# Attention into a token-and-channel mixer on one core: three numbers of the planner that orders TensorE's work

## The chip, the core and the metric

The kernel runs on one core of one Trainium2 chip. The time is that of the device, in microseconds, for one execution of the whole kernel; smaller is better. The number compared is the median of several executions. A core has TensorE (PE: matrix products), VectorE (DVE), ScalarE (ACT), GpSimd (POOL) and SyncE (SP). Here GpSimd issues the loads, SyncE issues the transposes made by DMA and the stores. Matrix products write to PSUM, which VectorE and ScalarE read; everything else lives in SBUF.

## The reference, cut to what matters

```python
# q, k, v: (8 batches, 12 heads, 448 rows, 64)
scores = scale * (q @ k.T) - log(448)
attn = 1 / (1 + exp(-scores))            # a sigmoid in place of a softmax
x = (attn @ v), heads side by side       # (8, 448, 768)
h = relu(x.T @ w_tok1) @ w_tok2          # token mixing: 448 -> 256 -> 448
u = x + h.T
h2 = relu(u @ w_ch1) @ w_ch2             # channel mixing: 768 -> 1536 -> 768
out = u + h2                             # float32
```

## The kernel before, in words

The eight batches run through the same steps. The names below are those of the planner's units, and the lines those of the profile.

*Attention* of a batch is three groups of four heads. The unit S (scores, L578: eight matmuls for a pair of units) is followed by a sigmoid on ScalarE (L594); V (values, L616, 28 matmuls) sums over the 448 keys. Scores and values use 64 x 64 tiles of the array. From batch 2 on, q and k are loaded by GpSimd, permuted (L496) and turned by a DMA transpose (L501), and the attention's result goes back to row order by a DMA transpose (L664, "x"; a part of batches 2 and 3 goes through TensorE, L675).

*Token mixing.* V1 and K1 (L841, L857) make the hidden layer, K2 and V2 (tok2, L933 and L891) the sum back over rows. VectorE adds x (L955, L923) and so makes u in float32. ScalarE casts each block of u to float16 (L963), and SyncE turns it with a DMA transpose into uT (L991); there are four of these for a batch, named uT_b_0 to uT_b_3, the last block shared by two batches.

*Channel mixing.* C1 (L1007) has 12 units of six matmuls of 448 columns, VectorE applies the relu (L1023). C2 (L1066) has six or eight units of twelve matmuls of 384 columns; VectorE adds u (L1079), SyncE stores (L1050, L1044). The first C1 unit of a batch, C1_b_0, needs all four uT of the batch, since a matmul of it takes all rows as the moving operand.

Each C1 and C2 unit is made of two halves, a first one and one whose name ends in "_h". Both write the same PSUM bank, so a unit is open until its second half is done. A unit is "broken" when other work stands between the halves.

*What sets the order.* A planner in the kernel's Python code (class Plan, L55 to L218) computes the order before the program is built. It keeps its own estimates of durations and of landing times, walks through time, and asks `choose` (L1153) at each step which unit TensorE takes next. `choose` gathers candidates that are ready by these estimates and takes the one with the lowest priority number: a group of scores that is due has 1, one not yet due has 5; the token units have 2, C1 has 3, C2 has 4, tails (V1, V2) 3.5. The first K2 of a pair has 4.5 while the counter `rest`, the microseconds of TensorE mixer work since the last K2, is under REST (L1197). A second half has its own number (L1201). When a score group is due is given by `due` (L1135): a share of the mixer work of the batch before, less LEAD microseconds. Engines then execute their own instructions in the order written; semaphores carry the true dependencies, so the planner's estimates decide the order alone and not when something may start.

Of the kernel before, what the change touches and what calls it, by code (L numbers as in the profile page):

```python
# [55 lines left out]
class Plan:  # L56
# [75 lines left out]
    def run(self, choose):  # L132

        lists = {}
        for o in self.ops:
            if o.engine != "PE":
                lists.setdefault(o.engine, []).append(o)
        free = dict.fromkeys([*lists, "PE", "POOL"], 0.7)
        free["POOL"] = 0.8
        mode = [None]  # L140
        self.left = len(self.ops)
        while self.left:
            best = None
            for e, ops in lists.items():
                if e == "LD":
                    ops = ops[:1]
                for o in ops:
                    r = self.ready(o)
                    if r is None:
                        continue  # L150
                    at = free[e]
                    if e == "LD":
                        at = max(free["POOL"], self.landed[-8])
                    key = (max(r, at), o.rank, r)
                    if best is None or key < best[0]:
                        best = (key, e, o)
            pick = choose(self, free["PE"])
            if pick is not None:
                t, ops, kind = pick
                if best is None or t <= best[0][0]:  # L160
                    for o in ops:
                        r = self.ready(o)
                        t = max(t, r, free["PE"])
                        if kind != mode[0]:
                            t += 0.1
                            mode[0] = kind
                        self.hold(o)
                        o.start, o.end = t, t + o.us
                        free["PE"] = t = o.end
                        self.log.append(o)  # L170
                        self.left -= 1
                    continue
            if best is None:
                raise RuntimeError(
                    "\n".join(
                        f"{o.name} <- {[d.name for d in o.after if d.end is None]}"
                        for o in self.ops
                        if o.start is None
                    )[:1500]
                )  # L180
            (t, _, _), e, o = best
            self.hold(o)
            o.start = t
            if e == "LD":
                far = self.load_far if self.pipe > 50.0 else 0.4
                free["POOL"] = t + o.n * o.issue
                self.pipe = max(self.pipe, free["POOL"] + 1.3) + o.us
                while self.hitch and self.pipe > self.hitch[0][0]:
                    self.pipe += self.hitch.pop(0)[1]
                o.end = self.pipe + far  # L190
                self.landed += [o.end] * o.n
            elif e == "SP":
                free[e] = t + o.us
                o.end = t + self.far + min(5.0, max(0.0, self.pipe - t - 0.5))
            else:
                o.end = free[e] = t + o.us
            lists[e].remove(o)
            self.log.append(o)
            self.left -= 1
        self.log.sort(key=lambda o: o.start)  # L200
        for o in self.log:
            o.emit()
# [3 lines left out]
def kernel(  # L206
# [23 lines left out]
    DH = D // 2  # L230
    att_scale = 1.0 / math.sqrt(E)
    att_bias = -math.log(S)
    LEAD, SPAN, REST, LATE = 20.0, 0.86, 0.8, 0
    FILL, UP, SURE = 21.0, 7, 0.8
    PACK, PACK2 = range(2, 8), range(2, 8)
    JOIN, PULL, ALONE = 0.05, 3.0, 3.5
# [898 lines left out]
    def due(g):  # L1135
        b, i, _ = g
        return -1.0 if b < 2 else base[b - 1] - LEAD + i * SPAN * mix[b - 1]

    def settle():
        c = state["chosen"]  # L1140
        state["chosen"] = None
        if c is None or c[2][0].start is None:
            return
        row = c[4]
        row.remove(c[5])
        if any(o.name[:3] == "V2_" for o in c[2]):
            state["rest"] = -PAUSE
        if row is not groups and c[2][0].name[0] != "V":
            o = c[2][0]
            state["done"] += o.us  # L1150
            state["rest"] = 0.0 if o.name[:2] == "K2" else state["rest"] + o.us

    def choose(plan, t):  # L1153
        settle()
        tails[:] = [o for o in tails if o.start is None]
        g = groups[0] if groups else None
        plan.spare = g is None or len(g[2]) < 3 or state["done"] < due(g) - 1.5
        cands = []
        want = groups[0][2] if groups and groups[0][0] and state["done"] >= due(groups[0]) else []
        late = [d.end for o in want for d in o.after]  # L1160
        short = want and None not in late and max(late) < t + 0.5 and want[0].name[0] == "V"
        for o in extra:
            r = plan.ready(o)
            if r is not None:
                cands.append((max(r, t), o.pri, [o], o.kind, extra, o))
        if groups:
            g = groups[0]
            r = plan.ready(*g[2])
            if r is not None:
                more = []  # L1170
                for o in tails[:3]:
                    r2 = plan.ready(*g[2], *more, o) if g[0] else None
                    if r2 is not None and r2 <= max(t, r) + JOIN:
                        more.append(o)
                        r = max(r, r2)
                p = -1 if g[0] == 0 else 1 if state["done"] >= due(g) - (PULL if more else 0) else 5
                cands.append((max(t, r), p, g[2] + more, "64", groups, g))
        if tails and (ALONE or not groups):
            alone = []
            for o in tails[:3]:  # L1180
                r = plan.ready(*alone, o)
                if r is not None and r <= t + 0.3:
                    alone.append(o)
            if alone:
                cands.append((max(t, plan.ready(*alone)), ALONE or 1.5, alone, "64", [0], 0))
        for rank, kinds in ((2, K), (3, C1), (4, C2)):
            n = 0
            for row in kinds:
                for o in row:
                    if o.name[:2] == "K2" and o.name[-1] == "1" and row.index(o) > 0 and row[row.index(o) - 1].name[:-1] == o.name[:-1]:  # L1190
                        n += 1
                        continue
                    r = plan.ready(o)
                    if short and rank == 2:
                        r = None
                    if r is not None:
                        p = 4.5 if o.name[:2] == "K2" and o.name[-1] == "0" and state["rest"] < REST else rank  # L1197
                        if o.name[:4] == "K2_0":
                            p = 3.5
                        if o.name[-2:] == "_h":  # L1200
                            p = 1.2  # L1201
                        cands.append((max(r, t), p, [o], "128", row, o))
                    n += 1
                    if n > (3 if rank == 2 else 0):
                        break
                if n > (3 if rank == 2 else 0):
                    break
        o = fill.get("op")
        if o is not None and o.start is None:
            plan.ops.remove(o)  # L1210
            uT[0].users.remove(o)
            plan.left -= 1
            fill["op"] = None
        if 3.0 < t < FILL and (not cands or min(c[0] for c in cands) > t + 0.12) and up.start is not None:
            if any(x <= t - SURE for x, _ in plan.free_slots("bank", up)):
                o = fill["op"] = filler()
                plan.left += 1
                state["chosen"] = (t, 0, [o], "128", [o], o)
                return t, [o], "128"
        if not cands:  # L1220
            return None
        first = min(c[0] for c in cands)
        cands = [c for c in cands if c[0] <= max(first, t) + 0.06]
        c = min(cands, key=lambda c: (c[1], c[0]))
        state["chosen"] = c
        return c[0], c[2], c[3]

    with tc.manual_schedule():
        plan.run(choose)
# [30 lines left out]
```

## Time and profile before

| | |
|---|---|
| median of 5 executions | 376.39 us |
| lowest and highest | 375.44 and 382.24 us |
| the profiled execution | 382.24 us, its span 380.4 us |
| granted TensorE clock in it | 0.986 of full speed |
| TensorE busy | 369.1 us (97%) |
| ScalarE, VectorE, GpSimd busy | 208.1, 175.6, 116.1 us |
| read from and written to HBM | 43.45 and 11.01 MB |

The profiled execution is the slowest of the five. The span runs from the first to the last instruction; the executions' time has some 1.8 us around it. A "busy" TensorE is not one at its peak, and shares of busy time are averages over stages with different limits. A wait names the engine or DMA that came last. In SyncE's rows a transpose's length is the time of issuing it, and the transfer lands later.

### The profile page before, as it was taken

How to read it: one execution, taken by the hardware profiler on the slowest of the kernel's cores; microseconds unless marked ns; L12 is line 12 of the kernel's file. 1: busy time of each engine (PE TensorE's matmuls, PEld its weight loads, DVE VectorE, ACT ScalarE, POOL GpSimd, SP SyncE). 2: the span in 40 equal slices, each digit the busy share in tenths (PEclk: the TensorE clock that was granted, in tenths of full speed). 3: DMA queues.
4: the chain of work that ended last, by engine and by line, in shares of the span. 5: the costliest groups of instructions: out<-in, count | busy, mean ns of one | idle time of the engine just before them, and what ended most of it. 6: DMA issues, size and time to landing. Idle time of an engine off the chain costs nothing.

```text
span 380.4 us, 7967 instructions
## 1 busy us (share of the span) xinstructions
PE 369.1 (97%) x3188; PEld 187.5 (49%) x3188; DVE 175.6 (46%) x414; ACT 208.1 (55%) x269; POOL 116.1 (31%) x261
## 2 busy tenths in 40 slices
PE   8799999999999999999699999999999999999995
PEld 4355345554444544455244555445455555555653
DVE  4366345743334644353124463664462257755222
ACT  5787993286777767788357576762665321200000
POOL 8882236234544435444424433440000000000000
PEclk9989999999999999999789999999999999999999
DMA  6999999499899989999989799994013563400344
GB/s 102 174 174 206 211 206 183 86 157 213 126 142 139 196 158 121 134 129 194 205 144 122 119 156 186 158 192 97 17 26 74 110 135 92 86 0 2 83 98 110
DMA packets 97013, 50.06 MB, mean 132 GB/s; under 512 B 70544, under 2 KB 93456, under 8 KB 96976
## 3 DMA queue, kind: packets, MB, share of 16 engines
q1 hardware_dynamic: 72656, 27.62, 40.8%
q0 software_dynamic: 24080, 21.62, 40.8%
q8 instruction: 25, 0.41, 0.5%
q10 hardware_dynamic: 240, 0.31, 0.2%
q14 instruction: 12, 0.10, 0.1%
HBM read 43.45 MB, written 11.01 MB: 143 GB/s over the span
## 4 chain that ended last, share of the span: by engine, by line
PE 92%; DMA 3%; POOL 2%; ACT 1%; DVE 0%; issue 0%; ACTq 0%; POOLq 0%
PE c L1007 30%; PE c L1066 29%; PE qk L578 11%; PE xa L616 8%; PE yn L933 4%; PE k L857 3%; DMA uT<-u 2%; DMA q<-in_q_dram 2%; POOL k L329 1%; PE xb L675 1%; PE k L707 1%; ACT attn L594 1%; POOL q L329 1%; PE k L817 1%; PE k L841 1%; PE tq L524 1%
## 5 line engine op out<-in xcount | busy, mean ns | idle before, releaser
L594 ACT ACTIVATE attn<-qk,att_bias 128x896 f16<-128x896 f32 (+1 forms) x172 | 161.8, 987 | 67.1 <-PE qk L578 66.3
L1007 PE MATMUL c<-uT,w_ch 128*128 128x448 f16 x576 | 121.8, 358 | 3.1 <-DMA uT<-u 3.1
L1066 PE MATMUL c<-w_ch,h2aT 128*128 128x384 f16 x576 | 100.0, 326 | 0.0
L1023 DVE TENSOR_SCALAR h2aT<-c 128x384 f16<-128x384 f32 x96 | 53.5, 557 | 85.0 <-PE c L1007 84.9
L1007 PEld LDWEIGHTS <-w_ch 128*128 128x128 f16 x576 | 53.1, 99 | 61.3 <-issue 15.4
L1066 PEld LDWEIGHTS <-h2aT 128*128 128x128 f16 x576 | 54.8, 98 | 40.6 <-issue 5.9
L1079 DVE TENSOR_TENSOR u<-u,c 128x384 f32<-128x384 f32 x48 | 26.6, 554 | 67.4 <-PE c L1066 67.1
L578 PE MATMUL qk<-qT,kT 64*64 64x448 f16 x672 | 54.3, 368 | 0.9 <-ACT attn L594 0.3
L781 POOL COPY mark<-attn 1x1 f16<-1x1 f16 x54 | 9.7, 180 | 91.7 <-ACT attn L594 91.6
L616 PE MATMUL xa<-attn,v 64*64 64x448 f16 x672 | 36.9, 351 | 0.0
L963 ACT ACTIVATE u<-u 128x768 f16<-128x768 f32 x21 | 17.7, 844 | 28.9 <-DVE u L955 28.7
L578 PEld LDWEIGHTS <-kT 64*64 64x64 f16 x672 | 14.8, 105 | 32.8 <-issue 30.7
L955 DVE TENSOR_TENSOR u<-x,yn 128x384 f32<-128x384 f16 x48 | 24.6, 548 | 4.8 <-PE yn L933 4.7
L496 POOL COPY kp<-k 128x384 f16<-128x384 f16 (+1 forms) x54 | 21.3, 429 | 16.9 <-DMA k<-in_k_dram 14.6
L653 ACT ACTIVATE xT<-xa 128x448 f16<-128x448 f32 (+2 forms) x61 | 22.2, 440 | 7.2 <-PE xa L616 5.7
L616 PEld LDWEIGHTS <-v 64*64 64x64 f16 x672 | 19.8, 108 | 12.2 <-issue 0.9
L496 POOL COPY qp<-q 128x384 f16<-128x384 f16 (+1 forms) x54 | 21.4, 433 | 8.5 <-DMA q<-in_q_dram 8.2
L933 PE MATMUL yn<-h,w_tok 128*128 128x384 f16 x104 | 21.6, 327 | 0.0
L1023 DVE TENSOR_SCALAR h2odd<-c 128x64 f16<-128x64 f32 x96 | 20.6, 214 | 0.0
L1066 PE MATMUL c<-w_ch,h2odd 128*128 128x384 f16 x96 | 17.1, 326 | 0.0
L340 POOL DMA_DIRECT2D q<-in_q_dram x21 | 15.1, 718 | 6.4 <-issue 5.3
L340 POOL DMA_DIRECT2D k<-in_k_dram x21 | 15.1, 719 | 4.7 <-issue 4.7
(73 smaller groups left out, 207.1 us busy)
## 6 DMA issues: line engine op xcount, KB each, us to landing
out_dram<-u SPq DMA_DIRECT2D x48, 192.0 KB, 3.1
k<-in_k_dram POOLq DMA_DIRECT2D x21, 224.0 KB, 5.1
q<-in_q_dram POOLq DMA_DIRECT2D x21, 224.0 KB, 5.5
v<-in_v_dram POOLq DMA_DIRECT2D x21, 224.0 KB, 5.5
w_ch<-in_moe_w_ch_dram POOLq DMA_DIRECT2D x6, 768.0 KB, 18.4
out_dram<-ut SPq DMA_DIRECT2D x6, 192.0 KB, 3.6
v<-in_v_dram POOLq DMA_DIRECT2D x6, 112.0 KB, 5.1
x<-xT SPq DMA_TRANSPOSE x32, 4.1
```

The source lines that it names most:

```text
L340: nc.gpsimd.dma_start(out=t.ap().rearrange("r h j e -> r h (j e)"), in_=heads.rearrange("(h s) (p j) e -> (s p) h (j e)", s=2, j=J),)
L496: nc.gpsimd.tensor_copy(out=pm[:, to, :, :], in_=src[:, fr, :, :])
L578: nc.tensor.matmul(out=ps[64 * s : 64 * s + 64, h, 0:S], lhsT=kT[64 * h : 64 * h + 64, i, s, :], rhs=qT[64 * h : 64 * h + 64, :, s, :], st ...
L594: nc.scalar.activation(out=at[:, hs, :], in_=ps[:, hs, 0:S], func=SIGMOID, bias=bias_t[:, :], scale=att_scale,)
L616: nc.tensor.matmul(out=ps[s](slice(64 * h, 64 * h + 64)), lhsT=vf[64 * s : 64 * s + 64, h, order[i], :], rhs=attn[i][64 * s : 64 * s + 64, ...
L653: nc.scalar.activation(out=xt[:, s, to : to + n], in_=ps[s](every)[:, fr : fr + n], func=COPYF)
L933: nc.tensor.matmul(out=ps[:, :], lhsT=w_tok2[:, t, s0 : s0 + 2, :], rhs=h1[b][:, t, c], start=(t == 0), stop=(t == 1),)
L955: nc.vector.tensor_tensor(out=to, in0=x, in1=y, op=ADD)
L1007: nc.tensor.matmul(out=ps[:, :], lhsT=w_ch1[cb // 4][:, db, 128 * (cb % 4) : 128 * (cb % 4) + 128], rhs=uT[b][:, db, :], start=(db == 0), ...
L1023: nc.vector.tensor_scalar(out=to, in0=ps[:, fr], scalar1=0.0, scalar2=None, op0=MAX)
L1066: nc.tensor.matmul(out=ps[:, :], lhsT=h, rhs=w, start=(cb == 0), stop=(cb == NCB - 1))
L1079: nc.vector.tensor_tensor(out=t, in0=t, in1=ps[:, :], op=ADD)
```

## The change

Three numbers of the planner and the length of an error text are changed. LEAD goes from 20 to 18, so that score groups fall due later by 2 us of mixer work. REST goes from 0.8 to 1.0. The priority of a second half goes from 1.2, ahead of all but due score groups, to 2.1, behind the token units (2) and ahead of the start of another C1 unit (3) or C2 unit (4).

```diff
@@ class Plan, run
-                    )[:1500]
+                    )[:200]
@@ the kernel's constants
-    LEAD, SPAN, REST, LATE = 20.0, 0.86, 0.8, 0
+    LEAD, SPAN, REST, LATE = 18.0, 0.86, 1.0, 0
@@ choose
                         if o.name[-2:] == "_h":
-                            p = 1.2
+                            p = 2.1
                         cands.append((max(r, t), p, [o], "128", row, o))
```

In the built program the orders of the engines are the same up to the ninth C1 unit of batch 2 and differ from there to the start of channel 2 of batch 6. The number of instructions of every engine stays.

## Prediction

> **What bounds the kernel now.** First the page: busy times and granted clock.
>
> ```profile
> PE 369.1 (97%) x3188; PEld 187.5 (49%) x3188; DVE 175.6 (46%) x414; ACT 208.1 (55%) x269; POOL 116.1 (31%) x261
> ...
> PEclk9989999999999999999789999999999999999999
> ```
>
> TensorE is the bound: 369.1 of 380.4 us, no other engine over 55%. In the clock row (slices of 9.5 us) the only digits below 9 after the start are a 7 and an 8, from 181 to 200 us. Next the waits of TensorE: the longest is
>
> ```profile
> PE c L1007 <- DMA uT<-u: 3.1, 1, 3.1
> ```
>
> All its others together are 4 us, none over 2. Then the chain that ended last, from 172 to 200 us (start, length, what):
>
> ```profile
> 174.89 1.95 PE c L1066 x12
> ...
> 177.34 1.32 PE xa L616 x28
> ...
> 180.54 6.31 DMA uT<-u
> ...
> 186.90 4.66 PE c L1007 x12
> 191.56 0.89 PE qk L578 x8
> 192.45 1.47 PE xa L616 x28
> ...
> 195.16 0.50 PE qk L578 x8
> 195.66 2.94 PE c L1007 x15
> ```
>
> The first channel-1 matmul of batch 3 (unit C1_3_0) stands still until the last of four transposes of u (uT_3_2) has landed, and the work after it is slow: twelve matmuls in 4.66, where 2.94 x 12/15 = 2.35 is the pace later. The table by stage gives the clock (last but two columns):
>
> ```profile
> 190.00:192.00 2.00, 2.00 (x13) 0.64 (x15) 0.45 (x2) 0.00 (x0) 0.00 (x0) 0.50 1.14 281
> ```
>
> Granted 0.50. Price of this one event: idle 3.11; slow matmuls 4.66 - 2.35 = 2.31, scores 0.89 - 0.50 = 0.39, values 1.47 - 1.32 = 0.15, together 2.85. Sum **5.96 us**. Last the reason: ACT's cast of that block, then SyncE's queue.
>
> ```profile
> 175.85 0.84 ACT L963 ACTIVATE u<-u 128x768 f16<-128x768 f32 x1
> ```
>
> ```profile
> 172.06 1.24 SPq L991 DMA_TRANSPOSE uT<-u  x1
> 173.39 1.25 SPq L501 DMA_TRANSPOSE qT<-qp  x1
> 174.73 1.22 SPq L991 DMA_TRANSPOSE uT<-u  x1
> 176.04 1.18 SPq L1050 DMA_DIRECT2D out_dram<-u  x2
> 177.31 1.29 SPq L991 DMA_TRANSPOSE uT<-u  x1
> 178.70 1.75 SPq L501 DMA_TRANSPOSE kT<-kp  x1
> 180.54 1.85 SPq L991 DMA_TRANSPOSE uT<-u  x1
> ```
>
> The cast ended at 176.69, the transpose started at 180.54: 3.85 us in the queue, behind a store, another block's transpose and a k transpose. It landed 6.31 later.
>
> **How this stands to the runs.** The profiled execution took 382.24 (span 380.4 and 1.8 around it); the median of five is 376.39. 382.24 - 5.96 = 376.28, within 0.11 of the median, so I read the median execution as one in which uT_3_2 came in time. This is inferred from the sum: only one execution has a profile.
>
> [...]
>
> **The change, part by part.** Three numbers of the planner change, and a length in an error text (nothing). What they do is read from the order of the built programs' instructions. TensorE has 6378 rows in each, DVE 403, ACT 273, POOL 220: nothing is added or removed, and changes between 64-row and 128-row units on TensorE are 222 in both. So the work itself costs **0**. What moves:
>
> 1. Second halves at 2.1 instead of 1.2: token units (rank 2) now go between the halves. From batch 3 on K1, V2 and K2 units come some units earlier; an opened unit holds its PSUM bank longer. Cost: if banks ran short, TensorE would wait for DVE. DVE is 46% busy and the trace has no TensorE wait on DVE after the first 2 us; the kernel before already parts S and V units between halves. 0; bounds -0.3 to +1.0 (one relu pair, 0.557 + 0.214 from the page, or two u sums of 0.548, late once).
> 2. REST 0.8 to 1.0: between two K2 pairs there is more than one channel-2 half (0.975 = 1.95/2), though units may now be parted; before, the unparted unit saw to that. DVE's additions (0.548 each) keep their room. 0.
> 3. LEAD 20 to 18: score groups fall due 2 us of mixer work later. They feed ACT, which has slack at 55%; loads of k, q, v gated by those (POOL) move with them. In the order no value unit comes closer to its load. 0.
>
> **Where it matters: the distance between a transpose's source and its user.** I add up TensorE's work between the last tok2 half of a batch and its C1 unit, with durations of the trace: channel-2 half 0.975, channel-1 half 0.57 (the chain has six matmuls of L1007 in 1.14), pair of scores 0.50, values 1.32, tok2 half 0.33.
>
> - Batch 3, before: 0.33 + 6 halves 5.85 + 3 x 0.50 + 1.32 = 9.0 (trace: from 174.40 to 183.79, 9.4). Needed: 174.40 to the landing at 186.85, 12.45. Short by 3.1. After: C2_2_2_1 (two halves) and two score pairs leave, but C2_2_0_1, C2_2_1_0 and others come in between: 0.33 + 8 x 0.975 + 1.50 + 1.32 = 10.95, or 11.3 with the trace's excess of 0.4. If the chain is as long as before, the wait is 12.45 - 11.3 = **1.1**. But SP's queue changes: the store of batch 2's first block (176.04 to 177.31, 1.27) and the k transpose (178.70 to 180.54, 1.84) now stand behind uT_3_2, and uT_3_0 and uT_3_1 (1.33 and 1.39) go before the k transpose of the unit before, where SP was idle from 159.75 to 163.62. That is 5.8 off the 3.85 in the queue. Against it: the two x transposes of batch 4 now stand just ahead (in the trace 167.67 to 171.96 for the two). Chain 8.6 to 12.45, available 11.3: wait 0 to 1.1, value taken 0.
> - Batch 4: needed 9.5 (225.37 to 234.88); there before 11.8, after 12.6. Batch 5: needed 6.0; 10.3, after 12.2. Both 0.
> - Batch 6: needed 5.1 (310.32 to 315.39); 9.5 before, after 8.5. Batch 7: needed 6.0 (324.81 to 330.80); 10.5 before, after 0.33 + 13 x 0.57 = 7.7. Closer, still 1.7 in hand.
> - The x transposes of batch 7 before V1_7_0: needed 5.4 (values end 298.93, last landing 304.36); 13.7 before, after 6 x 0.975 + 4 x 0.33 = 7.2. 1.8 in hand; no store stands directly ahead of them any more.
>
> The last 31 us (channel 2 of batches 6 and 7) keep their order, so the end is as before. C2_5_3_1 now follows the channel 1 of batch 7; its store has over 25 us of work to hide under.
>
> **Sum.** Against the profiled execution: 382.24 - 5.96 (event gone) + 0 = 376.28. Against the median: 0. I forecast **376.3**.
>
> **Rivals.** (a) Small waits: the batch 3 wait of up to 1.1, or C1_7_0 or V1_7_0 1 us late, without loss of clock: 377.3, up to 378.5. For it: these distances shrink. Against: each has 1.7 in hand. 0.14. (b) Slower: C1_3_0 still outruns uT_3_2. C1 goes ahead of C2_2_2_1 as soon as the planner thinks the data there, [...]. It costs as before, 376.3 + 5.96 = 382.2, once the chain exceeds 11.3 + 3.1 = 14.4, 2 us more than the bad execution showed; from 15 us it is over 1% in every run. 0.12. (c) The median before holds a small wait at this place that goes: lowest run 375.44, so 375.4; 0.12. Over 1% faster would be 372.6, which needs 3.7 us of idle time that a median run hasn't got: idle is 11.3 in all, of which the start holds most; only a measurement in which the kernel before itself mostly falls into the wait could show it, 0.07. (d) The orders differ, but nothing measurable does: this is my forecast itself, 0.55.
>
> **Numbers.** 1% (3.8 us) is about what a measurement of this kernel tells from no change. Within 1%: forecast 0.55, (a) 0.14, (c) 0.12: 0.81. Slower 0.12; faster 0.07. Range: from 375.0 (c, with the spread of the lower runs) to 379.0 (a, and part of b); forecast alone 375.4 to 377.3.
>
> **What would show it.** TensorE's waits without L1007 on uT; clock 1.00 from 180 to 200; SP's rows with two u transposes ahead of the store of ut near 160; equal busy work; no wait of L841 on x near 305 or of L1007 near 333. It is wrong if a wait of over 3 us for a transpose shows anywhere, or if TensorE waits for DVE banks where token units now part the halves.

## The result, and the profile after

The changed kernel takes 374.06 us (median of 43 executions, 373.60 to 377.89). The kernel before takes 376.36 (median of 80, 374.04 to 382.24). The ratio is 0.9938, 95% interval 0.9924 to 0.9952: faster by 0.6%, 2.3 us. The forecast was 376.3 with a range of 375.0 to 379.0; it said that nothing would change, and the result lies 0.9 below the range. The ratios here and below are taken from the fast executions alone, and need not be the quotients of the medians given beside them.

The spreads differ as much as the medians. Of the 80 executions of the kernel before only two are under 374.5; of the 43 of the kernel after, 37 are.

The page of the kernel after, busy times and granted clock:

```profile
PE 365.1 (98%) x3188; PEld 185.8 (50%) x3188; DVE 176.0 (47%) x414; ACT 208.3 (56%) x269; POOL 116.1 (31%) x261
...
PEclk9999999999999999999999999999999999999999
```

The same 3188 matmuls, and the dip of the clock near 185 us is gone (mean granted clock 1.000, against 0.986 in the profile before). The longest waits of TensorE (who waited for whom, us in total, times, longest) are now

```profile
PE idle L463 <- DVE att_bias L276: 1.2, 1, 1.2
PE tq L524 <- DMA q<-in_q_dram: 0.6, 1, 0.6
```

both in the first 16 us; the wait of L1007 for uT isn't in the list. SyncE's queue of the kernel after (start, length of the issue, what):

```profile
157.08 3.33 SPq L991 DMA_TRANSPOSE uT<-u  x2
160.51 1.26 SPq L501 DMA_TRANSPOSE kT<-kp  x1
163.37 1.18 SPq L991 DMA_TRANSPOSE uT<-u  x1
164.65 1.70 SPq L1044 DMA_DIRECT2D out_dram<-ut  x2
...
170.85 1.27 SPq L991 DMA_TRANSPOSE uT<-u  x1
172.21 1.18 SPq L1050 DMA_DIRECT2D out_dram<-u  x2
173.50 2.16 SPq L501 DMA_TRANSPOSE kT<-kp  x1
```

Three of the four transposes of u (157.08, twice, and 163.37) go out before the store of ut, where the prediction had two, and uT_3_2 (170.85) goes ahead of the store and the k transpose that stood ahead of it before. It landed 4.05 us later, at 174.90. TensorE comes to C1_3_0 at 178.04, without a wait (timeline of TensorE: start, length, what):

```profile
176.62 1.49 PE L616 MATMUL xa<-attn,v 64*64 64x448 f16 x28
178.04 1.31 PE L1007 MATMUL c<-uT,w_ch 128*128 128x448 f16 x6
```

The rest is as the prediction drew it. What it had wrong is how much of the same event a typical execution of the kernel before pays.

**A measure that leaves the start out.** Up to about 146 us all the kernels here execute the same instructions; only that of run 6 departs earlier, near 70 us. For every profile I take from the trace the stretch from the first C1_0_0 matmul (near 37 us) to the start of the last channel-2 half, C2_7_3_1_h:

| profile | C1_0_0 begins | stretch | wait at C1_3_0 |
|---|---|---|---|
| before | 39.60 | 335.70 | 3.11, granted clock 0.50 after it |
| the order before, in run rest_only | 37.02 | 333.64 | 2.12, granted clock 0.50 after it |
| after | 37.33 | 329.89 | 0 |
| after, once more (run after_again) | 42.69 | 329.90 | 0 |

The profile before had thus lost time twice: 335.70 - 329.89 = 5.81 at the event, and 39.60 - 37.33 = 2.27 at its start. The profiled executions took 382.24 and 374.13; of these 8.11 us, 8.08 are the two.

### The profile page after: what moved, and what is told of

The parts are those of the page before. It is cut to its first block, busy times and chain, and to the rows that moved or that the text cites. A ratio compares the mean times of both kernels' runs of the same rounds, so it can differ in the third digit from the quotient of the medians.

```text
span 372.4 us, 7968 instructions
## 1 busy us (share of the span) xinstructions
PE 365.1 (98%) x3188; PEld 185.8 (50%) x3188; DVE 176.0 (47%) x414; ACT 208.3 (56%) x269; POOL 116.1 (31%) x261
## 4 chain that ended last, share of the span: by engine, by line
PE 94%; POOL 2%; DMA 1%; DVE 1%; ACT 1%; issue 0%; ACTq 0%; POOLq 0%
PE c L1007 30%; PE c L1066 30%; PE qk L578 11%; PE xa L616 9%; PE yn L933 5%; PE k L857 4%; DMA v<-in_v_dram 1%; PE xb L675 1%; POOL k L329 1%; PE k L817 1%; PE k L841 1%; PE k L707 1%; PE tq L524 1%; POOL q L329 1%; PE tk L524 1%; PE yt L891 1%
## 5 line engine op out<-in xcount | busy, mean ns | idle before, releaser
L1007 PE MATMUL c<-uT,w_ch 128*128 128x448 f16 x576 | 119.0, 353 | 0.0
L1007 PEld LDWEIGHTS <-w_ch 128*128 128x128 f16 x576 | 52.8, 98 | 56.4 <-issue 12.7
L578 PE MATMUL qk<-qT,kT 64*64 64x448 f16 x672 | 53.5, 363 | 0.7 <-ACT attn L594 0.3
L496 POOL COPY kp<-k 128x384 f16<-128x384 f16 (+1 forms) x54 | 21.3, 430 | 14.5 <-DMA k<-in_k_dram 11.3
L870 DVE TENSOR_SCALAR h<-k 128x384 f16<-128x384 f32 x24 | 12.7, 557 | 9.8 <-PE k L857 9.8
```

What stands on the lines that cost most here:

```text
L496: nc.gpsimd.tensor_copy(out=pm[:, to, :, :], in_=src[:, fr, :, :])
L578: nc.tensor.matmul(out=ps[64 * s : 64 * s + 64, h, 0:S], lhsT=kT[64 * h : 64 * h + 64, i, s, :], rhs=qT[64 * h : 64 * h + 64, :, s, :], st ...
L1007: nc.tensor.matmul(out=ps[:, :], lhsT=w_ch1[cb // 4][:, db, 128 * (cb % 4) : 128 * (cb % 4) + 128], rhs=uT[b][:, db, :], start=(db == 0), ...
```

## The experiments

Two theories, stated ahead of the first runs. **W**: most executions of the kernel before pay a wait at C1_3_0 for uT_3_2, and the change takes it away. **O**: the gain comes from TensorE's new order itself. S and L, in the expectations, are side questions: whether the wait is rare, and whether LEAD matters.

**1. REST alone.**

```diff
-    LEAD, SPAN, REST, LATE = 20.0, 0.86, 0.8, 0
+    LEAD, SPAN, REST, LATE = 20.0, 0.86, 1.0, 0
```

> REST alone, 1.0 instead of 0.8. The order of every engine is that of the kernel before, instruction for instruction, so the time is that of the kernel before in every theory (ratio 1.00). It is run for its profile, a second look at an execution of the order before. Theory W (a wait at C1_3_0 is in most executions of the order before): L1007 waits for uT at the first channel-1 unit of batch 3, some 1 to 3 us near 182 us, while the waits of the start add up to no more than in the kernel after. Theory S (the start differs from execution to execution and the wait at C1_3_0 is rare): no wait of L1007 on uT.

Measured: 377.55 (374.67 to 379.73), the kernel before beside it 376.08, ratio 1.0009 (0.9981 to 1.0036). The program is that of the kernel before, instruction for instruction, so the 1.5 us between the two medians is what one program varies by. The profiled execution took 377.59. Its wait for uT, and its chain around 183 us (start, length, what):

```profile
PE c L1007 <- DMA uT<-u: 2.1, 1, 2.1
```

```profile
176.76 6.51 DMA uT<-u
...
183.32 4.13 PE c L1007 x12
187.45 0.50 PE qk L578 x8
```

The transpose took 6.51 to land, TensorE stood for 2.12, and the twelve matmuls after it took 4.13 instead of 2.35. The waits of this profile show nothing for a load of q at the start. So this is an execution without the start's loss and still 3.5 us above the kernel after. Theory S falls, W stands.

**2. The kernel before, two entries of SyncE's queue moved.** TensorE's order stays that before.

```diff
-        self.log.sort(key=lambda o: o.start)
+        self.log.sort(key=lambda o: next(x.start for x in self.ops if x.name == "uT_3_2") + 0.01
+                      if o.name in ('st_2_0', 'turnk_5_2') else o.start)
```

> The kernel before with SyncE's order alone changed: the store st_2_0 and the k transpose turnk_5_2 stand behind uT_3_2 instead of ahead of it. TensorE, ACT, DVE and POOL keep the order before. Theory W: uT_3_2 issues about 3 us earlier, the wait at C1_3_0 goes or shrinks to under 1 us, and the time comes down to 374.0 to 374.8 (ratio 0.994 to 0.997), most of what the change brings. Theory O (the gain is in TensorE's new order itself, fewer short gaps between units, and not in this wait): unchanged, 376.4, ratio 1.00.

Measured: 373.96 (373.46 to 376.72), ratio 0.9932 (0.9903 to 0.9962). This is the whole gain of the change, with no unit of TensorE moved. SyncE's queue in it:

```profile
171.32 4.04 SPq L991 DMA_TRANSPOSE uT<-u  x3
175.46 1.18 SPq L1050 DMA_DIRECT2D out_dram<-u  x2
176.74 1.70 SPq L501 DMA_TRANSPOSE kT<-kp  x1
```

The third of these transposes is uT_3_2, issued at 174.15; it landed at 177.89, and C1_3_0 began at 181.15 without a wait. The stretch is 329.76, against 329.89 of the kernel after: TensorE's new order by itself is worth nothing that shows. Theory O falls.

**3. The kernel before, only the store moved.** The edit is that of 2 with one name in the list.

```diff
+                      if o.name in ('st_2_0',) else o.start)
```

> The kernel before with one entry of SyncE's queue moved: the store st_2_0 stands behind uT_3_2, the k transpose turnk_5_2 stays ahead of it. Theory W (the wait at C1_3_0 is what separates the two kernels) says: half of the move that brought 373.96. In the profile of REST alone the wait was 2.12 us, and the store took 1.27 of the queue, so the wait falls to about 1 us in such an execution and to nothing in milder ones; time 374.3 to 375.5. Theory O (TensorE's order) says 376.1.

Measured: 373.99 (373.61 to 375.36), ratio 0.993 (0.9904 to 0.9956). The median lies 0.3 under the expected span: moving one store by one place is enough in most executions. The profiled one (374.81) still waited:

```profile
PE c L1007 <- DMA uT<-u: 0.9, 1, 0.9
```

**4 and 5. The kernel after, uT_3_2 put back.** In the first it stands behind the store st_2_0, the k transpose turnk_5_2 and the store st_2_1; in the second (turnk_5_2 in the place of st_2_1 in the edit) not behind st_2_1.

```diff
-        self.log.sort(key=lambda o: o.start)
+        self.log.sort(key=lambda o: next(x.start for x in self.ops if x.name == "st_2_1") + 0.01
+                      if o.name in ('uT_3_2',) else o.start)
```

> The kernel after with SyncE's order alone changed: uT_3_2 stands behind st_2_0, turnk_5_2 and st_2_1, so it issues near 176.5 instead of 170.85 and lands near 181, where TensorE reaches C1_3_0 at 178.0. Theory W: a wait of 2.5 to 4 us comes back at C1_3_0, with or without half clock after it; time 376.5 to 379.5, ratio to the kernel before 1.00 to 1.01. Theory O: SyncE's order has no say in the gain, 374.1, ratio 0.994.

> The kernel after with uT_3_2 behind st_2_0 and turnk_5_2, not behind st_2_1. It should issue near 174 and land near 178.5, where TensorE arrives at 177.8 to 178.0. Theory W: a wait of 0 to 1 us, no loss of clock; time 374.1 to 375.2. Theory O: 374.1.

Measured: 377.54 (376.30 to 378.63), ratio 1.0019 (0.9986 to 1.0051), and 375.42 (374.20 to 377.64), ratio 0.998 (0.9956 to 1.0003). The gain is lost altogether in the first, and more than half of it in the second, 0.2 above what was expected: there uT_3_2 issued at 174.40, took 5.16 to land, and TensorE waited 1.71, where 0 to 1 was expected. The chain of the first:

```profile
175.88 4.56 DMA uT<-u
180.44 0.14 issue
180.58 1.29 PE c L1007 x6
```

Here the wait was 2.74, and the matmuls behind it went at full speed: the granted clock is 1.00 in every stretch of 2 us from 174 to 198. Median and profile of this run differ (377.54, 376.63); other executions of it have a mean granted clock of 0.993 to 0.995.

**6. The priority alone.**

```diff
                         if o.name[-2:] == "_h":
-                            p = 1.2
+                            p = 2.1
```

> The priority of second halves alone, 2.1, with LEAD 20 and REST 0.8. uT_3_2 then issues early and the last of batch 3's four transposes is uT_3_3. Theory W: the wait at C1_3_0 depends on how far the last transpose stands ahead of C1_3_0: by the order it is a little closer than in the kernel after, so 374.1 to 375.5, ratio 0.994 to 0.998. Theory O: the parted halves alone bring the gain, 374.1, ratio 0.994.

Measured: 376.58 (374.95 to 380.12), ratio 1.0008 (0.998 to 1.0036). Neither theory had this. There is no wait at C1_3_0 (172.64), yet the stretch is 331.81. Two waits came up at the first channel-1 units of batches 4 and 5 (TensorE's timeline; idle time in brackets, then what is named as its end):

```profile
231.23 2.05 PE L1007 MATMUL c<-uT,w_ch 128*128 128x448 f16 x10 [0.45 <-ACT attn L594]
...
255.90 1.30 PE L1007 MATMUL c<-uT,w_ch 128*128 128x448 f16 x6 [0.48 <-DMA uT<-u]
```

ScalarE is named at the first, but uT_4_2 landed at 231.14, 0.09 before the start; at the second uT_5_2 landed at 255.77. A third wait, 0.44 near 127.9, is for VectorE's addition to ut. Together 1.37 of the 1.92 by which the stretch exceeds that of the kernel after; the other 0.55 can't be placed, since this order is its own from 70 us on and wasn't run without the waits. So the priority alone mends batch 3 and moves the trouble to the batches behind it.

**7. The priority and REST, without LEAD.** The edit of 6 and REST 1.0.

> The priority 2.1 and REST 1.0 with LEAD still 20. Around C1_3_0 the order is that of the kernel after, eleven units' work between the last tok2 half and C1_3_0 and uT_3_2 ahead of st_2_0 and turnk_5_2. Theory W: no wait at C1_3_0, 374.0 to 374.6, ratio 0.994 to 0.996, so that these two numbers are the effective part. Theory L (LEAD is needed): 375 to 377.

Measured: 373.70 (373.41 to 374.63), ratio 0.9942 (0.9919 to 0.9964), 0.3 below what was expected. No wait for uT in this profile; uT_3_2 landed at 174.73, C1_3_0 began at 177.91. The effective part of the change is this pair.

**8. LEAD alone.**

```diff
-    LEAD, SPAN, REST, LATE = 20.0, 0.86, 0.8, 0
+    LEAD, SPAN, REST, LATE = 18.0, 0.86, 0.8, 0
```

> LEAD 18 alone. Score groups move, but from the last tok2 unit of batch 3 to C1_3_0 TensorE's units and SyncE's queue ahead of uT_3_2 are as before. Theory W: the wait at C1_3_0 stays, 376 to 377, ratio 1.00; TensorE's work and order at other places differ and may add some tenths. Theory L (the later score groups bring the gain): 374.1, ratio 0.994.

Measured: 376.42 (375.21 to 380.58), ratio 1.0011 (0.9989 to 1.0034), with a wait of 1.01 at C1_3_0 in the profile. The profiled execution took 380.58, the highest of its run: its C1_0_0 began at 42.47, 5.1 us later than in the kernel after. LEAD by itself does nothing that shows.

**9 and 10. The kernel after and the version without LEAD on one chip.**

> The kernel after once more, on the same chip as the next one: 374.0 plus or minus 0.3, ratio to the kernel before 0.993 to 0.996, no wait for uT at C1_3_0 in its profile.

> Priority 2.1 and REST 1.0 without LEAD, to be set beside the kernel after on one chip. If LEAD 18 costs something, this one is 0.2 to 0.4 below the kernel after (373.7 was measured on another chip); if LEAD does nothing, the two are within 0.15.

Measured: 374.14 (15 executions), ratio 0.9945 (0.9923 to 0.9966), and 373.58 (10 executions), ratio 0.9926 (0.99 to 0.9952). The version without LEAD is 0.56 below in the medians, a little more than expected, and it was the lower one on another chip too (373.70). But its stretches are 329.54 and 330.27, those of the kernel after 329.89 and 329.90; the second of its profiles even has a wait of 0.58 for uT at C1_5_0 that the kernel after hasn't got. So the profiles don't show where it would gain. The version without LEAD beats the kernel before; that it beats the kernel after stays open.

**What a wait at C1_3_0 costs**, from five profiles. The excess is the stretch less that of the same kernel's order without the wait (329.76 for the orders before, 329.89 for those after):

| run | wait | excess of the stretch | granted clock after it |
|---|---|---|---|
| before_store_late | 0.87 | 0.94 | 1.00 |
| after_late1 | 1.71 | 1.77 | 1.00 |
| after_late_uT | 2.74 | 2.79 | 1.00 |
| rest_only | 2.12 | 3.88 | 0.50 for 3.4 us |
| before | 3.11 | 5.94 | 0.50 for 6.8 us |

In the three profiles at full clock the excess is the wait and 0.05 to 0.07 more. In the two with a granted clock of 0.50 it is the wait and 1.76 or 2.83 more. (lead_only, with waits of 1.07 in a stretch of 331.17, is left out: its order wasn't run without them.)

## Why the prediction was wrong

**The step that failed** is the one headed "How this stands to the runs": "382.24 - 5.96 = 376.28, within 0.11 of the median, so I read the median execution as one in which uT_3_2 came in time." The price of the event was right: the prediction had 5.96, and 335.70 - 329.76 is 5.94. The conclusion from it was not. The profiled execution had lost another 2.27 us at the start. Its sign stood in the list of waits that the prediction read, the line after the event's (here of the kernel before):

```profile
PE tq L524 <- DMA q<-in_q_dram: 2.0, 2, 1.8
```

and was put aside with "All its others together are 4 us, none over 2." A second sign stood in the clock row that it shows, an 8 in the third slice: behind the longer of these two waits, 1.83 us, the clock was halved from 18.54 to 21.96 us. Whether this wait belongs to every execution, one profile can't tell; it is absent from the second profile of the same order (rest_only), whose C1_0_0 starts at 37.02 instead of 39.60. With both taken off, 382.24 - 5.96 - 2.27 = 374.01, and the changed kernel measured 374.06. So the floor of the order before was 374.0 and its median, 376.36, contains 2.3 us of the very wait. The agreement to 0.11 came from two errors of like size: a start's loss left in, and a typical wait taken as none. Against it also stood the spread: 375.44 to 382.24 in five executions is what a wait of varying length would do.

**Rival (c)** had the right mechanism, "The median before holds a small wait at this place that goes". It was priced at 0.9, from the lowest of five executions as a floor, and given 0.12. It measures 2.3; among 80 executions the lowest is 374.04.

The granted clock recorded with each execution carries this to those without a profile. Beside the experiments the kernel before ran 131 times, on three chips. In 93 of them the mean clock was 0.997 or more; their medians, 375.6 to 375.9 by chip, still lie 1.5 to 1.8 above the kernel after. In the other 38 it was 0.996 or less, with medians from 377.9 to 378.4. Of the kernel after no execution, and of run 3 none of 14, was at 0.996 or less. This fits a typical execution of the kernel before that pays the wait alone, and, as an estimate from the 38 of 131, about three in ten that pay half clock too.

Point by point, the rest:

- *The work costs nothing, and nothing in TensorE's order does.* Right: 329.76 with the order before and no wait, 329.89 with the order after.
- *Batch 3: 11.3 us available, 8.6 to 12.45 needed, wait taken as 0.* Right in the wait: 174.90 - 166.77 = 8.13 needed, 178.04 - 166.77 = 11.27 there. The 8.13 lies below the span for a reason that the sum had not: it kept the landing at 6.31, and it took 4.05. The queue still cost 1.5 (the cast ended at 169.34, the issue began at 170.85); the "5.8 off the 3.85 in the queue" can't be more than 3.85. What goes first in SyncE's queue decides it, as worked out; runs 2 to 5 show it from both sides.
- *The distances of batches 6 and 7 and of V1_7_0 shrink but hold.* Right: no wait for a transpose is in the list after. Rival (a), a small wait there, and rival (b), a wait of 6 us, didn't come.
- *REST costs 0.* Right only for REST alone, which changes no instruction's place. Beside the priority of 2.1 it isn't free: without it 376.58, with it 373.70. The prediction argued with VectorE's room; in p_only two of the three waits were for a transpose of u again.
- *LEAD costs 0.* Right: 1.0011 (0.9989 to 1.0034).
- *Parted units hold PSUM banks longer, 0.* Right: after the first 40 us the profile after has no wait of TensorE for VectorE.
- *"1% (3.8 us) is about what a measurement of this kernel tells from no change."* Too coarse: the interval measured is 0.0014 to each side, 0.5 us.
- *The idle time that a median execution hasn't got.* The statement that over 1% was out of reach held; the gain is 0.6%. But "the start holds most" of the 11.3 us idle was no bound on what a median execution loses at the event.

**Half clock and wait.** The table by stage of the kernel before (clock in the last column but two):

```profile
185.50:186.00 0.50, 0.00 (x0) 0.00 (x0) 0.00 (x0) 0.11 (x1) 0.50 (x1) 0.80 1.36 72
...
192.50:193.00 0.50, 0.50 (x13) 0.23 (x8) 0.00 (x0) 0.50 (x1) 0.00 (x0) 0.88 0.99 215
```

The trace's clock records have 0.50 from 185.79 to 192.62 us. It set in 2.0 us after TensorE had stopped at 183.8 and lasted 6.8. In rest_only, with a wait of 2.12, it set in 2.2 us after the stop and lasted 3.4. The wait of 2.74 in after_late_uT brought none, nor did those of 1.71 and 0.87. So the length of the wait alone doesn't tell whether half clock follows; what does isn't shown by these profiles.

## What to carry to other kernels

A profile is one execution: before its time less one event is set equal to a median, account for every other loss in it against a second profile, and take a wide spread of the times (here 374.04 to 382.24) as a sign that the event is frequent and of varying length. Here, with TensorE busy 97% of the span, moving one or two entries of SyncE's queue (373.99 and 373.96) did what three retuned numbers of the planner did (374.06), and TensorE's own order did nothing that shows (stretches of 329.76 and 329.89). So ask for each transfer that TensorE will wait for what stands ahead of it in its queue, and whether a store or a later load's transpose could go behind.

## What was not expected

**The start differs from execution to execution.** The instructions up to C1_0_0 are the same in all the kernels, and C1_0_0 began between 37.02 and 42.69 us in the profiles, in eight of the twelve by 37.33. In the kernel before (39.60) and in p_only (39.98) there is a wait of 1.8 or 2.1 us for a load of q; in the kernel before half clock stood behind it, from 18.54 to 21.96 us, and p_only has a mean granted clock of 0.994. In after_again (42.69) and lead_only (42.47) no such wait is there; in after_again the scores at 11 us took 0.58 for two matmuls, where the profile after has 0.38 (first the one, then the other):

```profile
11.10 0.58 PE L578 MATMUL qk<-qT,kT 64*64 64x448 f16 x2
```

```profile
10.46 0.38 PE L578 MATMUL qk<-qT,kT 64*64 64x448 f16 x2
```

The views show a granted clock of 1.00 there, but only because no clock record covers that time. The trace's first record, of full clock, begins at 20.82 us in after_again and at 20.73 in lead_only, and between 4.0 and 6.8 in the ten other profiles. The pace of after_again changes at this very place:

```profile
19.85 0.59 PE L578 MATMUL qk<-qT,kT 64*64 64x448 f16 x4
...
21.07 0.38 PE L578 MATMUL qk<-qT,kT 64*64 64x448 f16 x4
```

So after_again kept the slower pace, 0.58 or 0.59 against 0.38, to about 20 us; that lead_only did too is inferred from its first clock record and its late C1_0_0. Why isn't settled; in after_again TensorE was busy for 4.35 us of the stretch from 5 to 10 us and for all of that from 10 to 20.

**A transpose's landing is far from constant.** uT_3_2 took 3.74 to 6.51 us from issue to landing in the profiles above, a range wider than the wait in question. It doesn't look like chance alone. In the five profiles in which a k transpose stands directly ahead of it in SyncE's queue (before, rest_only, before_store_late, lead_only, after_late1) it took 5.16 to 6.51; in the six in which a store or a transpose of u or x stands there (before_sp_order, after, after_again, p_rest, p_rest_again, after_late_uT) 3.74 to 4.56. These runs differ in more than the neighbour, so the cause isn't shown; that a k transpose moved behind is worth landing time as well as queue time is an estimate from these two ranges. Nor is the landing all that varies: between the two profiles of the order before it differs by 0.2, and the issue, counted from C1_0_0, by 1.2 (180.54 - 39.60 = 140.94, 176.76 - 37.02 = 139.74). The 3.1 us of room in the kernel after (178.04 - 174.90) take in both.
